# Attention and MLP kernel: keys and queries transposed by DMA from cast copies in DRAM, both halves of a head pair in one unit

## The chip, the cores and the metric

The kernel runs on one core of a Trainium2 chip. The metric is the device time of one execution in microseconds (us), the median over runs. Engines are named as in the profile: PE (TensorE, matmul), PEld (its weight loads), DVE (VectorE), ACT (ScalarE), POOL (GpSimd), SP (SyncE, which here only issues DMA transfers).

## The reference

```python
B, H, S, D = 8, 8, 576, 64            # q, k, v: float32
window = 32                           # 8 global tokens besides
mask = |pos_i - pos_j| <= window, or i global, or j global
attn = softmax(where(mask, q @ k.T / sqrt(D), -1e9))
x = (attn @ v).transpose(0, 2, 1, 3).reshape(4608, 512)
h = maximum(x @ w_in, 0)              # w_in 512 x 2048
out = (h * h) @ w_out                 # w_out 2048 x 512, float32 out
```

## The kernel before

A unit of attention is one pair of heads of one batch: 8 batches times 4 pairs, index `i = 4*b + hp`. Its 576 queries, with the 8 global queries repeated after each 144, make 608 columns; they are cut into two halves of 304. The keys stand in five tiles of 120 rows, each led by the 8 global keys. `WIN` lists for each half the windows (key tile, place in the score tile, first column, width) that the mask leaves: five in the first half, of which two have 8 columns and serve the global queries alone, and three in the second.

For one half, `scores` multiplies keys and queries into `sc` and takes the exponential on ACT; in batches 0 and 1 the mask is added by a matmul of `far` with the identity ahead of the scores, later it is a product on DVE (`er` to `et`). `pv` multiplies by the values and by ones into `acc` (sums beside outputs; in batches 0 and 1 in column tiles of 64), takes 1/sum on ACT as exp(-ln(sum)), and writes the scaled outputs to `xT` on DVE. The global queries' outputs of all four pairs are gathered in `gx`, and `scatter` copies them on POOL to their columns of `xT`, eight copies per batch.

Keys and queries come in natural order by `fetch_pair` (SP) in float32 to `st`, are cast to fp16 (`cast_tokens`, DVE and ACT) and transposed on PE with the identity (`transposed`), six transposes for each of k and q of a unit; DVE copies the result to `kt` and `qt`. Values come in float32 and are cast too (`cast_values`). The rows of global tokens come by an indirect DMA for two batches at a time (`gather_rows`), go to a DRAM scratch and from there under the tokens.

The MLP works on chunks of 512 tokens (columns of `xT`): `mm1` is one unit of four matmuls 128x512 with `w_in`, a relu on ACT and a square on DVE; `mm2` is a quarter of one output tile, four matmuls with `w_out`; after four quarters DVE copies `ot` and SP stores it. Chunk 0 has its first layer in two halves of 256 tokens (`mm1_half`, eight units each).

The order on every engine is the order in which the program is written. MLP units are laid between attention steps by `fill` and `take` from the list `fills`. Three PSUM buffers `mm`, one each of `sc`, `acc` and `tr`. Batch 0 runs all its first halves, then all second halves; from batch 2 on each half step has about two MLP units before and after the outputs of the half before. The last two chunks run alone at the end.

Of the kernel before, what the change touches and what calls it, by code (L numbers as in the profile page):

```python
# [17 lines left out]
KT = 120  # L18
NT = 5
# [15 lines left out]
SCW = (456, 440)  # L35
MB = (0, 456)
NBUF = 5
# [3 lines left out]
def kernel(  # L41
# [33 lines left out]
    bufs_of = {"sc": 1, "acc": 1, "tr": 1, "mm": 3}  # L75

# [3 lines left out]
    st = {nm: sbt("st" + nm, [TP + NG, H, TJ, D], FP32) for nm in "kq"}  # L80
    st["v"] = sbt("stv", [P, NT, H, D], FP32)
    kts = [sbt(f"kt{i}", [P, NT, P], FP16) for i in range(NBUF)]
    qts = [sbt(f"qt{i}", [P, NCOL], FP16) for i in range(NBUF)]

    vts = [sbt(f"vt{i}", [P, NT, 3, D], FP16) for i in range(NBUF)]
# [7 lines left out]
    nc.scalar.preload_act_table_set("natural_log_exp_and_others")  # L93


    g64 = sbt("g64", [1, NG], I64)
    src = {"k": k, "q": q, "v": v}
    gscr = {}

    def fetch_tokens(eng, nm, b, hp):  # L100
        hs = slice(2 * hp, 2 * hp + 2)
        eng.dma_start(
            out=st[nm][0:TP, hs].rearrange("p h j d -> p h (j d)"),
            in_=src[nm][b, hs].rearrange("h (p j) d -> p h (j d)", j=TJ),
        )

    def fetch_values(eng, b, hp):
        hs = slice(2 * hp, 2 * hp + 2)
        dst = st["v"]
        for h in range(2 * hp, 2 * hp + 2):  # L110
            eng.dma_start(
                out=dst[8 : 8 + KT, 0:4, h],
                in_=v[b, h, 0 : 4 * KT].rearrange("(t s) d -> s t d", s=KT),
            )
        eng.dma_start(
            out=dst[8 : 8 + KN[4], 4, hs], in_=v[b, hs, 4 * KT : S].rearrange("h s d -> s h d")
        )

    def fetch_globals(b, hp):
        def rows(nm):  # L120
            return gscr[(nm, b // 2)][b % 2, :, 2 * hp : 2 * hp + 2]


        for nm in "kq":
            js = range(TJ) if b == 2 else (TJ - 1,)
            for h in range(2):
                dst = st[nm][TP : TP + NG, 2 * hp + h, js[0] : TJ]
                nc.sync.dma_start(
                    out=dst, in_=rows(nm)[:, h].unsqueeze(1).to_broadcast((NG, len(js), D))
                )  # L130
        nc.sync.dma_start(
            out=st["v"][0:NG, :, 2 * hp : 2 * hp + 2].rearrange("p t h d -> p t (h d)"),
            in_=rows("v").rearrange("g h d -> g (h d)").unsqueeze(1).to_broadcast((NG, NT, 2 * D)),
        )

    fetch_tokens(nc.sync, "k", 0, 0)
    nc.scalar.dma_start(out=g64, in_=global_idx.unsqueeze(0))
    fetch_tokens(nc.scalar, "q", 0, 0)
    fetch_tokens(nc.scalar, "q", 0, 1)
    fetch_tokens(nc.sync, "k", 0, 1)  # L140
    fetch_values(nc.sync, 0, 0)
    fetch_values(nc.sync, 0, 1)
    fetch_tokens(nc.sync, "k", 0, 2)
    fetch_tokens(nc.sync, "q", 0, 2)
    fetch_values(nc.sync, 0, 2)
    fetch_tokens(nc.sync, "k", 0, 3)
    fetch_tokens(nc.sync, "q", 0, 3)
    fetch_values(nc.sync, 0, 3)


    idle = sbt("idle", [P, 512], FP16)
    nc.vector.memset(idle, 0.0)
    ones = sbt("ones", [1, P], FP16)
    nc.vector.memset(ones, 1.0)
    nc.scalar.copy(
        out=st["v"][0:NG].rearrange("p t h d -> p t (h d)"),
        in_=idle[0:NG].unsqueeze(1).to_broadcast((NG, NT, H * D)),
    )
    pidx = sbt("pidx", [P, 4], I32)
    nc.gpsimd.iota(pidx, pattern=[[0, 4]], base=0, channel_multiplier=1)  # L160
# [714 lines left out]
```

## Time and profile before

| | us |
|---|---|
| runs (three): median, lowest, highest | 371.36, 371.32, 372.39 |
| profiled execution: span, first to last instruction | 368.4 |
| PE busy / DVE busy / ACT busy / POOL busy | 347.7 / 250.5 / 249.2 / 51.3 |
| DMA: moved, mean rate | 43.93 MB, 119 GB/s |

The page gives for the profiled execution its own span and no separate time; the median of the runs lies 2.96 us above the span. Busy times of the engines overlap. A row of a timeline has the start, the busy time, the engine, the line and what was written from what; a matmul's busy time includes its passage through the array, so the price of a group on PE is read from the distance of starts. Names such as `mm<-xT,w_in` are output and inputs. In a table by stage the columns are the stage, its length, busy time of PE, PEld, DVE, ACT and POOL with instructions in brackets, the granted clock of PE, the DMA engines' busy share and GB/s.

### The profile page before, as it was taken

What the parts mean: (1) busy time and instruction counts of PE and PEld (TensorE: products, weight loads), DVE (VectorE), ACT (ScalarE), POOL (GpSimd) and SP (SyncE); (2) the same over time, 40 slices, a digit from 0 to 9 for tenths busy, and PEclk for the clock granted to TensorE, in tenths of its full rate; (3) what the DMA queues carried; (4) which work ended last, traced back from release to release, by engine and by line L of the source; (5) the groups of instructions that cost most, each with busy time, mean ns of one, the idle gap of its engine ahead of it and who ended that gap; (6) DMA issues with size and microseconds to landing.
All of it is one profiled execution on the core that took longest, in us unless ns stands there. A gap on an engine that the chain in (4) does not pass through costs nothing.

```text
span 368.4 us, 8258 instructions
## 1 busy us (share of the span) xinstructions
PE 347.7 (94%) x2941; PEld 186.0 (51%) x2941; DVE 250.5 (68%) x656; ACT 249.2 (68%) x482; POOL 51.3 (14%) x143
## 2 busy tenths in 40 slices
PE   7779799988899999999999999999999989999995
PEld 3556575544445555555555555555555544444442
DVE  7753566656888878977897789778977953422421
ACT  6656574465997799679967996799679942612610
POOL 5364430016000610020002000200020001000000
PEclk9978999998999999999999999999999999999999
DMA  8999999787843663375336533652020011002002
GB/s 196 192 147 201 193 228 201 188 188 193 188 130 97 188 166 94 90 188 142 95 93 187 142 95 93 187 140 60 30 87 2 0 52 64 0 30 85 0 32 85
DMA packets 65011, 43.93 MB, mean 119 GB/s; under 512 B 42730, under 2 KB 60074, under 8 KB 64970
## 3 DMA queue, kind: packets, MB, share of 16 engines
q1 hardware_dynamic: 59752, 38.03, 40.0%
q0 software_dynamic: 4800, 4.79, 7.9%
q10 hardware_dynamic: 418, 0.59, 0.7%
q8 instruction: 23, 0.38, 0.5%
q14 instruction: 18, 0.15, 0.1%
HBM read 37.85 MB, written 9.73 MB: 129 GB/s over the span
## 4 chain that ended last, share of the span: by engine, by line
PE 60%; issue 14%; DVE 7%; DMA 6%; ACT 5%; POOL 4%; POOLq 2%; ACTq 0%; SPq 0%; DVEq 0%
PE mm L502 25%; PE mm L460 24%; PE acc L602 4%; PE tr L415 3%; DMA w_in<-in_moe_w_in_dram 3%; PE sc L564 3%; DVE gt L466 2%; DMA stq<-in_q_dram 2%; POOLq L649 2%; ACT rl L465 2%; DMA stv<-in_v_dram 1%; POOL xT L658 1%; ACT er L570 1%; ACT natq L386 1%; DVE et L574 1%
## 5 line engine op out<-in xcount | busy, mean ns | idle before, releaser
L502 PE MATMUL mm<-w_out,gt 128*128 128x512 f16 x576 | 133.6, 379 | 0.0
L460 PE MATMUL mm<-xT,w_in 128*128 128x512 f16 x512 | 120.7, 382 | 1.0 <-POOL xT L658 1.0
L465 ACT ACTIVATE rl<-mm 128x512 f16<-128x512 f32 x128 | 72.2, 595 | 34.6 <-PE mm L460 33.9
L502 PEld LDWEIGHTS <-gt 128*128 128x128 f16 x576 | 53.1, 97 | 55.6
L460 PEld LDWEIGHTS <-w_in 128*128 128x128 f16 x512 | 47.7, 98 | 51.2 <-issue 2.9
L612 ACT ACTIVATE rec<-acc 64x288 f32<-64x288 f32 (+1 forms) x112 | 45.5, 406 | 33.9 <-PE acc L602 24.1
L638 DVE TENSOR_TENSOR xT<-acc,rec 64x288 f16<-64x288 f32 (+1 forms) x112 | 50.9, 454 | 19.8 <-ACT rec L613 18.0
L466 DVE TENSOR_TENSOR gt<-rl 128x512 f16<-128x512 f16 x128 | 50.2, 421 | 18.2 <-ACT rl L465 17.5
L658 POOL COPY xT<-gx 128x4 f16 (+2 forms) x80 | 21.8, 272 | 231.1 <-DVE xT L638 226.8
L570 ACT ACTIVATE er<-sc 128x912 f16<-128x912 f32 (+1 forms) x48 | 44.0, 917 | 5.4 <-PE sc L564 5.0
L574 DVE TENSOR_TENSOR et<-er,mask 128x912 f16<-128x912 f16 (+1 forms) x48 | 29.9, 623 | 21.2 <-ACT er L570 20.9
L508 DVE COPY ot<-mm 128x512 f32<-128x512 f32 x36 | 24.9, 691 | 26.0 <-PE mm L502 25.3
L613 ACT ACTIVATE rec<-rec 128x288 f32<-128x288 f32 x64 | 28.3, 443 | 2.0
L386 ACT CAST natq<-stq 104x768 f16<-104x768 f32 (+1 forms) x32 | 26.4, 824 | 4.4 <-DMA stq<-in_q_dram 4.4
L570 ACT ACTIVATE et<-sc 128x912 f16<-128x912 f32 (+1 forms) x16 | 14.6, 915 | 12.0 <-PE sc L564 11.7
L386 DVE CAST natk<-stk 104x768 f16<-104x768 f32 (+1 forms) x32 | 17.7, 552 | 0.3
L479 PE MATMUL mm<-xT,w_in 128*128 128x256 f16 x128 | 16.8, 290 | 0.6 <-POOL xT L658 0.6
L479 PEld LDWEIGHTS <-w_in 128*128 128x128 f16 x128 | 12.7, 104 | 3.3 <-issue 0.6
L617 DVE TENSOR_REDUCE gs<-acc 128x16 f32<-128x32 f32 x32 | 6.0, 187 | 12.2 <-ACT rec L612 12.2
L415 PE MATMUL tr<-identity,natk 96*128 96x96 f16 x168 | 12.1, 208 | 1.9 <-DVE natk L386 1.8
L415 PEld LDWEIGHTS <-natq 96*128 96x128 f16 x192 | 9.2, 98 | 7.1 <-ACT natq L386 1.5
L491 DVE TENSOR_TENSOR gt<-rl 128x512 f16<-128x512 f16 x16 | 6.8, 426 | 8.4 <-ACT rl L490 8.1
(205 smaller groups left out, 324.2 us busy)
## 6 DMA issues: line engine op xcount, KB each, us to landing
stk<-in_k_dram SPq DMA_DIRECT2D x32, 288.0 KB
out_dram<-ot SPq DMA_DIRECT2D x36, 256.0 KB
stq<-in_q_dram SPq DMA_DIRECT2D x30, 288.0 KB
stv<-in_v_dram SPq DMA_DIRECT2D x64, 120.0 KB
w_in<-in_moe_w_in_dram POOLq DMA_DIRECT2D x4, 512.0 KB, 9.5
w_out<-in_moe_w_out_dram POOLq DMA_DIRECT2D x4, 512.0 KB, 9.0
stv<-in_v_dram SPq DMA_DIRECT2D x32, 48.0 KB
stq<-in_q_dram ACTq DMA_DIRECT2D x2, 288.0 KB
```

Source lines behind the costliest of these rows:

```text
L386: op(out=nat[0:n].rearrange("p j (h d) -> p h j d", d=D), in_=st[nm][0:n, 2 * hp : 2 * hp + 2],)
L415: nc.tensor.transpose(tr[:, TP * j : TP * j + n], nat[0:n, j, :], identity[0:n, 0:n])
L460: nc.tensor.matmul(ph, w_in[:, t, u * P : (u + 1) * P], xT[:, t, XOFF + c * TC : XOFF + (c + 1) * TC], start=(t == 0), stop=(t == NDM - 1),)
L465: nc.scalar.activation(out=rl, in_=ph, func=AF.Relu)
L466: nc.vector.tensor_tensor(out=gts[c][:, u, :], in0=rl, in1=rl, op=ALU.mult)
L479: nc.tensor.matmul(ph[:, j], w_in[:, t, (u + j) * P : (u + j + 1) * P], xT[:, t, half * (256 + XOFF) : half * (256 + XOFF) + 256], start=( ...
L502: nc.tensor.matmul(po, gts[c][:, f, m * P : (m + 1) * P], w_out[:, f, :], start=(f == 0), stop=(f == NFF - 1),)
L570: nc.scalar.activation(out=er[:, :, 0:W], in_=sc[:, :, 0:W], func=AF.Exp, bias=0.0, scale=scale)
L574: nc.vector.tensor_tensor(out=et[:, :, 0:W], in0=er[:, :, 0:W], in1=mask[:, MB[half] : MB[half] + W].unsqueeze(1).to_broadcast((P, 2, W)), ...
L612: nc.scalar.activation(out=rec[r], in_=av[rs, xs, :, 0:GTOK], func=AF.Ln)
L613: nc.scalar.activation(out=rec, in_=rec, func=AF.Exp, scale=-1.0)
L638: nc.vector.tensor_tensor(out=xT[r, hp, x0 : x0 + HS].rearrange("p (k x) -> p k x", k=2), in0=av[r, x, :, 0:GTOK], in1=rec[r], op=ALU.mult,)
```

## The change

Windows, names and lines below are the changed kernel's. What it does:

- Batches 2 to 7: POOL issues casting transfers (float32 read, fp16 written). `tokens_to_scratch` rewrites keys and queries of a batch in DRAM in the padded order (five and four transfers, pieces of 64 numbers), `globals_to_scratch` puts the gathered global rows between them, and `transposes` (SP) brings them with two transposing transfers to `kb` and `qb`. The PE transposes, the casts and the copies to `kt` and `qt` are gone there. `values` fetches and casts values straight to `vb` (five transfers). All this for batch b+1 is written after the first unit of batch b; POOL reaches it when its scatter of batch b-1 is done.
- Batch 1: keys and queries come cast to `nat` by POOL and are transposed on PE, 12 transposes of one head each for each of k and q. Batch 0 loads keys and queries by SP alone, values cast by POOL.
- `WIN2` leaves the two 8-column windows out: from batch 1 on (and in batch 0's second half, where nothing changes by it) both halves have three windows. The global queries' sums are taken in both halves and added (`gsh`), so that `gx` follows the second half.
- The mask is a product on DVE, in place, except in batch 0's first half.
- `unit`: scores of both halves (PSUM `sc` and `acc`), both exponentials, both products, then MLP units, outputs of the first half into `sc`, MLP, outputs of the second into `acc`, MLP. Batch 0's first half runs all scores, then all outputs.
- The column numbers of the scatter are loaded by three instructions instead of 24; weights are no longer gated behind other transfers; the gather of batches 0 and 1 is issued before w_out.

ACT, in one stretch of the batches with MLP. Before (batch 2, first and second half of a pair):

```order
L465 ACTIVATE rl<-mm 128x512 x2
L612 ACTIVATE rec<-acc 64x288 x2
L613 ACTIVATE rec<-rec 128x288
L465 ACTIVATE rl<-mm 128x512 x2
L570 ACTIVATE er<-sc 128x2x440
L465 ACTIVATE rl<-mm 128x512 x2
L612 ACTIVATE rec<-acc 64x288 x2
L613 ACTIVATE rec<-rec 128x288
L465 ACTIVATE rl<-mm 128x512 x2
L386 CAST natq<-stq 104x2x6x64
L394 CAST vt_80<-stv 128x4x2x64
L394 CAST vt_80<-stv 104x2x64
```

And now, ACT over one whole unit (a pair, both halves) of batch 2:

```order
L592 ACTIVATE et<-sc 128x2x440
L592 ACTIVATE et<-acc 128x2x440
L492 ACTIVATE rl<-mm 128x512 x2
L648 ACTIVATE rec<-sc 64x288 x2
L649 ACTIVATE rec<-rec 128x288
L492 ACTIVATE rl<-mm 128x512
L648 ACTIVATE rec<-acc 64x288 x2
L649 ACTIVATE rec<-rec 128x288
L492 ACTIVATE rl<-mm 128x512 x4
```

The casts are gone, and the two exponentials stand back to back ahead of the unit's relus.

SP, the transfers between two stores of outputs in batch 2, before (one pair's loads, of which there are four a batch):

```order
L102 DMA stk<-in_k_dram 96x2x384
L102 DMA stq<-in_q_dram 96x2x384
L111 DMA stv<-in_v_dram 120x4x64 x2
L115 DMA stv<-in_v_dram 96x2x64
L128 DMA stk<-gscr_k_1964 8x64 x2
L128 DMA stq<-gscr_q_1966 8x64 x2
L131 DMA stv<-gscr_v_1968 8x5x128
L510 DMA out_dram<-ot 128x512 x2
```

And now, SP for a whole batch (`scr` is the DRAM copy, `gst` the gathered rows):

```order
L378 DMA scr_k_710<-gstk 64x5x64
L378 DMA scr_q_713<-gstq 64x4x64
L355 DMA gscr_v_2047<-gstv 64x64
L401 DMA_TRANSPOSE kb<-scr_k_710 128x4x640
L401 DMA_TRANSPOSE qb<-scr_q_713 128x4x608
L410 DMA vb_77<-gscr_v_2047 8x8x64 x5
L537 DMA out_dram<-ot 128x512 x4
```

The stores of a chunk now stand behind the next batch's transposing transfers, which wait for POOL's.

POOL, around the scatter of batch 0's second half, with the semaphores that each waits for (DMASW: an earlier POOL transfer in the same of eight lanes). Before, ahead of it:

```order
L735 COPY xT<-xT 128x4x32 [waits Pool_49]
L754 COPY w_out<-w_in 1x1 [waits DMASW3_49,Pool_49]
L756 DMA w_out<-in_moe_w_out_dram 128x4x512 [waits Pool_49]
L756 DMA w_out<-in_moe_w_out_dram 128x4x512 x3
L649 TENSOR_LOAD g32b [waits DVE_49]
```

And now, up to that scatter's first copy (`vb_689` is batch 1's values):

```order
L761 COPY xT<-xT 128x4x32 [waits Pool_49]
L106 DMA natk<-in_k_dram 96x4x384 [waits DMASW0_49]
L106 DMA natq<-in_q_dram 96x4x384 [waits DMASW1_49]
L106 DMA natk<-in_k_dram 96x4x384 [waits DMASW2_49]
L106 DMA natq<-in_q_dram 96x4x384 [waits DMASW3_49]
L341 DMA gstk<-in_k_dram,gidx 128x64 [waits DMASW4_49]
L341 DMA gstq<-in_q_dram,gidx 128x64 [waits DMASW5_49]
L341 DMA gstv<-in_v_dram,gidx 128x64 [waits DMASW6_49]
L113 DMA vb_689<-in_v_dram 120x8x64 [waits DMASW7_49]
L113 DMA vb_689<-in_v_dram 120x8x64 [waits DMASW0_49]
L695 ISA
L695 COPY xT<-gx 128x4 [waits DVE_49,Pool_49]
```

The lanes go round: the last transfer here waits for the first `natk` of the same list, and the copy stands behind it. The weights' transfers lie ahead of all these in POOL's queue.

The diff, cut to what the prediction speaks of:

```diff
+WIN2 = (
+    ((0, 0, 0, 160), (1, 160, 88, 192), (2, 352, 216, 88)),
+    ((2, 0, 304, 112), (3, 112, 344, 192), (4, 304, 472, 136)),
+)
...
+    pool, dve, act = nc.gpsimd, nc.vector, nc.scalar
+    nat = {nm: sbt("nat" + nm, [TP + NG, H, TJ, D], FP16) for nm in "kq"}
...
+    def fetch_values(b, x, hs=slice(0, H)):
+        back = NG if b == 0 and x else 0
+        pool.dma_start(
+            out=vb[b][NG - back : NG + KN[x], x, 2 * hs.start : 2 * hs.stop : 2],
+            in_=v[b, hs, x * KT - back : x * KT + KN[x]].rearrange("h s d -> s h d"),
+        )
...
+    def globals_to_scratch(b):
+        for nm in "kq":
...
+            nc.sync.dma_start(
+                out=dst.rearrange("x g h d -> (g h) x d"),
+                in_=gathered(nm, b).unsqueeze(1).to_broadcast((NG * H, n, D)),
+            )
+        store_rows("v", b)
+
+    def tokens_to_scratch(b):
+        for nm in "kq":
+            n, step, pitch, off = {"k": (NT, KT, P, NG), "q": (4, GTOK, GRP, 0)}[nm]
+            for x in range(n):
+                lo, hi = x * step, min((x + 1) * step, S)
+                pool.dma_start(
+                    out=scr[(nm, b % 2)][x * pitch + off : x * pitch + off + hi - lo].rearrange(
+                        "s (h d) -> s h d", d=D
+                    ),
+                    in_=src[nm][b, :, lo:hi].rearrange("h s d -> s h d"),
+                )
+
+    def transposes(b):
+        for nm, d_, w in (("k", kb, KW), ("q", qb, QW)):
...
+            nc.sync.dma_start_transpose(out=d_[b], in_=scr[(nm, b % 2)][:, :])
...
+    def weights(half, sc, wins, added=False):
+        W = sum(x[3] for x in wins[half])
+        et = sbt("et", [P, 2, SCW[0]], FP16, bufs=4)
+        act.activation(
+            out=et[:, :, 0:W], in_=sc[:, :, 0:W], func=AF.Exp, bias=0.0, scale=scale
+        )
+        if not added:
+            dve.tensor_tensor(
+                out=et[:, :, 0:W], in0=et[:, :, 0:W],
...
-    for half in range(2):
-        for u in range(0, NFF, 2):
-            fills.append((8 * half + 8, 2, mm1_half, (u, half)))
+    half1(0)
+    half1(1)
+    for i in range(0, NHP, 2):
+        for nm in "kq":
+            fetch_tokens(pool, nm, 1, i, 2)
...
+    gather(1)
+    globals_to_scratch(2)
+    for x in range(2):
+        fetch_values(1, x)
+    keep_warm(4)
+    half1_out(0)
+    half1_out(1)
+    queue += units[0]
+    take(2)
+    half1(2)
+    half1(3)
+    take(2)
+    half1_out(2)
+    take(1)
+    half1_out(3)
+    take(3)
     scatter(0, 1)
+    for x in range(2, NT):
+        fetch_values(1, x)
+    tokens_to_scratch(2)
+    transposes(2)
...
+    queue += units[1] + units[2]
+    take(6)
...
+    def unit(i, n, nxt=None):
+        scs = [scores(i, half, pair_tag[half], WIN2) for half in range(2)]
+        et = [weights(half, scs[half], WIN2) for half in range(2)]
+        take(n[0])
+        if nxt:
+            tr_k(nxt, tag="tr", tail=act.copy)
+            tr_q(nxt, tag="mm", op=act.copy)
         for half in range(2):
+            acc = outputs(i, half, et[half], pair_tag[half], WIN2, columns=i < 2 * NHP)
+            finish_outputs(i, half, acc, columns=i < 2 * NHP)
+            if half == 0:
+                take(n[1])
+        if i % NHP == NHP - 1:
+            scatter(i // NHP)
+        take(n[2])
+
+    for hp in range(NHP):
+        unit(NHP + hp, (1, 1, 2) if hp < NHP - 1 else (1, 1, 2), NHP + hp + 1 if hp + 1 < NHP else None)
+    take(99)
+    for b in range(2, B):
+        queue += units[b + 1]
+        for hp in range(NHP):
+            unit(NHP * b + hp, ((2, 1, 4), (2, 1, 4), (2, 1, 5), (2, 1, 7))[hp])
+            if hp == 0 and b + 1 < B:
+                if b > 2 and b % 2:
+                    gather((b + 1) // 2)
+                globals_to_scratch(b + 1)
+                tokens_to_scratch(b + 1)
+                transposes(b + 1)
+                vb[b + 1] = vb[(b + 1) % 2]
+                values(b + 1)
+                value_globals(b + 1)
+        take(99)
+    queue += units[B + 1] + units[B + 2]
+    take(999)
```

More of the change, by code (lines that the diff above doesn't have):

```diff
@@ L136 @@
[L136 to L148, printed above, removed]
+            fetch_tokens(nc.sync, nm, 0, hp)
@@ new lines, in mask_first, with scores @@
+    def mask_first(half, tag):
+        sc = pst(tag, [P, 2, 512])
+        W = SCW[half]
+        for e in range(2):
+            nc.tensor.matmul(
+                sc[:, e, 0:W], identity, far[:, 0:W],
+                start=True, stop=False, skip_group_check=True,
+            )
+        return sc
+    def scores(i, half, tag, wins, sc=None):
+        kt, qt = key_query(i)
+        added = sc is not None
+        if not added:
+            sc = pst(tag, [P, 2, 512])
+        for t, so, c0, w in wins[half]:
@@ new lines, with half1, half1_out @@
+    scatter(0, 0)
+    pool.tensor_copy(out=xT[:, :, XOFF + 256 : XOFF + HS], in_=xT[:, :, 256:HS])
+    def half1(i):
+        tag = pair_tag[i % 2]
+        ets[i] = weights(1, scores(i, 1, tag, WIN2), WIN2)
+    def half1_out(i):
+        acc = outputs(i, 1, ets[i], pair_tag[i % 2], WIN2, columns=True)
+        finish_outputs(i, 1, acc, columns=True)
+    half1(0)
+    half1(1)
+    for i in range(0, NHP, 2):
+        for nm in "kq":
+            fetch_tokens(pool, nm, 1, i, 2)
+    vb[1] = sbt("vb1", [P, NT, 2 * H, D], FP16)
```

576 lines of the change are left out of this document (243 added, 333 removed).

## The prediction

> **What bounds the kernel now.** I read the page's busy line first, then a table by stage, then TensorE's own order of time in one steady stretch, then the chain that ended last.
>
> ```profile
> PE 347.7 (94%) x2941; PEld 186.0 (51%) x2941; DVE 250.5 (68%) x656; ACT 249.2 (68%) x482; POOL 51.3 (14%) x143
> PE 60%; issue 14%; DVE 7%; DMA 6%; ACT 5%; POOL 4%; POOLq 2%; ACTq 0%; SPq 0%; DVEq 0%
> 159.00:196.00 37.00, 36.73 (x307) 19.27 (x305) 30.67 (x77) 30.66 (x61) 2.53 (x9) 1.00 0.50 132
> 158.78 2.90 POOL L658 COPY xT<-gx 128x4 f16 x8 [26.88 <-DVE xT L638]
> 195.68 2.89 POOL L658 COPY xT<-gx 128x4 f16 x8 [33.99 <-DVE xT L638]
> ```
>
> In the stage 159 to 196 TensorE (PE) is busy 36.73 of 37.00 us, VectorE (DVE) and ScalarE (ACT) some 30.7, and the DMA engines half. The scatters of two neighbouring batches lie 36.90 us apart: that is one batch, and TensorE sets it. Here is what it runs in it; the start of a row less the start of the one before is that one's price.
>
> ```profile
> 171.82 0.40 PE L564 MATMUL sc<-qt_76,kt_71 64*128 64x160 f16 x10
> 172.15 0.43 PE L415 MATMUL tr<-identity,natk 96*128 96x96 f16 x6
> 172.42 1.89 PE L460 MATMUL mm<-xT,w_in 128*128 128x512 f16 x8
> 174.15 0.54 PE L602 MATMUL acc<-et,vt_80 128*128 128x112 f16 x6
> 174.53 1.91 PE L460 MATMUL mm<-xT,w_in 128*128 128x512 f16 x8
> 176.37 0.36 PE L564 MATMUL sc<-qt_76,kt_71 64*128 64x112 f16 x6
> 176.67 0.43 PE L415 MATMUL tr<-identity,natq 96*128 96x96 f16 x6
> 176.94 1.89 PE L460 MATMUL mm<-xT,w_in 128*128 128x512 f16 x8
> 178.67 0.63 PE L602 MATMUL acc<-et,vt_81 128*128 128x160 f16 x10
> 179.15 1.89 PE L460 MATMUL mm<-xT,w_in 128*128 128x512 f16 x8
> ```
>
> Eight MLP matmuls cost 1.73 us, so a unit of four costs 0.866. Scores cost 0.33 (ten matmuls) and 0.30 (six), outputs 0.48 and 0.38, six transposes 0.27. A pair of heads takes 0.33+0.30+0.48+0.38+0.54 = 2.03 us, four pairs 8.1; 32 MLP units 27.7; together 35.8 of 36.9.
>
> **The steady batches (2 to 7).** The transposes leave TensorE, and both halves have six matmuls, so a pair costs 2x0.30+2x0.38 = 1.36 us and a batch 4x1.36+27.7 = 33.1. Next I ask what is late then. A pair with seven first-layer units costs TensorE 7x0.866+1.36 = 7.42 us. ACT's rows, and one of a last output:
>
> ```profile
> 167.04 1.07 ACT L465 ACTIVATE rl<-mm 128x512 f16<-128x512 f32 x2
> 168.00 0.91 ACT L570 ACTIVATE er<-sc 128x880 f16<-128x880 f32 x1
> 168.85 0.60 ACT L465 ACTIVATE rl<-mm 128x512 f16<-128x512 f32 x1
> 170.34 0.82 ACT L612 ACTIVATE rec<-acc 64x288 f32<-64x288 f32 x2
> 171.19 0.44 ACT L613 ACTIVATE rec<-rec 128x288 f32<-128x288 f32 x1
> 171.54 0.58 ACT L465 ACTIVATE rl<-mm 128x512 f16<-128x512 f32 x1
> ...
> 192.78 0.55 PE L602 MATMUL acc<-et,vt_82 128*128 128x112 f16 x6
> ```
>
> By starts: exponential 0.85, relu 0.48, a pair of logarithms 0.85, reciprocal 0.35. The pair costs ACT 2x0.85+7x0.48+2x0.85+2x0.35 = 7.46: even with TensorE. ACT starts the two exponentials only after the last relu of the pair before, so I allow 0.35 us of waiting to each of the two such pairs: 7.8. The other two pairs hold 8 and 10 units, mostly second-layer ones without a relu: 8.3 and 10.0. A batch is 2x7.8+8.3+10.0 = 33.9 us. The casts of queries, keys and values leave ACT and DVE, which wait on TensorE there, and count nothing. The scatter now follows both halves: from the end of a last output (192.78+0.55) to the scatter (195.68) it is 2.35 us now, on ACT and DVE, and 2.90 on POOL; seven units, 6.1 us, and the next scores, 0.6, cover these 5.25. Without that cover they would be lost in each batch.
>
> **What feeds them.** For each batch from 2 on POOL issues 14 casting transfers: nine that rewrite keys and queries in fp16 in DRAM, 9216 pieces of 256 bytes read and 128 written, and five of values, 4608 pieces. SP then issues two transposing transfers of 1.28 MB in all. No row shows either kind; these are the nearest.
>
> ```profile
> q1 hardware_dynamic: 1642, 0.42, 120.8%
> q0 software_dynamic: 1639, 1.63, 123.3%
> L705 POOL DMA_DIRECT2D w_in<-in_moe_w_in_dram x4: 755/851/1246, 18.6 to 21.5; - x4
> L756 POOL DMA_DIRECT2D w_out<-in_moe_w_out_dram x4: 750/759/770, 33.3 to 35.5; - x4
> L375 POOL DMA_DIRECT2D gscr_k_1067<-gstk x1: 580/580/580, 49.8 to 49.8; - x1
> DMA packets 3378, 2.00 MB, mean 249 GB/s; under 512 B 2477, under 2 KB 3315, under 8 KB 3378
> ```
>
> The first row is the stretch 7 to 9 us, nearly all 256-byte pieces of values: 821 a us with all engines busy. The second is 22 to 30 us, weights cast from 2048 to 1024 bytes: 205 a us. The last is 48 to 56 us, at 249 GB/s. By these 13,824 pieces take 16.8 us at the first pace and 67 at the second. I take the first: its pieces read the same 256 bytes, the second row's eight times as many. The transposes take 5.1 us at 249 GB/s, and 24 as 4992 pieces of 256 bytes at the weights' pace; I take 5.1, the row nearest in mixed sizes. The four outputs of a batch (1.05 MB) take 4.2, the copies of global rows 0.7. Sum 26.8 of 33.9 us: hidden. On POOL an issue costs 0.58 us for 128 pieces and 0.76 for 512, 0.5 ns a piece; for about 990 pieces 1.0, so 14 cost 14 us, which start right behind the scatter and end 15 us before the next. The keys' transfers should land some 9 us into a batch and the queries' 14; if the transposes are late, the next batch's scores wait, and so do the output stores queued behind them on SP. SP itself issues 15 transfers a batch instead of 40. The Trainium skill (DMA: Bandwidth & Descriptors, "Latency and other measured facts") gives a transposing transfer 261 GB/s, by which the pair would be an estimated 4.9 us and the sum 26.6; no run here shows it yet.
>
> **The front.** The second chunk's MLP begins at 84.19 us now. These rows price the way to it:
>
> ```profile
> 26.46 4.27 PE L479 MATMUL mm<-xT,w_in 128*128 128x256 f16 x24 [0.64 <-POOL xT L658]
> 49.80 0.57 PE L594 MATMUL acc<-et,vt_82 128*64 128x112 f16 x12
> 50.31 3.67 PE L479 MATMUL mm<-xT,w_in 128*128 128x256 f16 x32
> 53.81 1.03 PE L502 MATMUL mm<-w_out,gt 128*128 128x512 f16 x4
> 84.19 3.54 PE L460 MATMUL mm<-xT,w_in 128*128 128x512 f16 x8 [0.99 <-POOL xT L658]
> 40.56 2.87 POOL L658 COPY xT<-gx 128x4 f16 x8 [4.28 <-DVE xT L638]
> ```
>
> The new thing there is a wait on POOL. Every POOL transfer waits for the eighth transfer before it (POOL's rows in the part on the change), so the second transfer of batch 1's values waits for the first one of batch 1's keys, which stands behind both weights in the same queue, and the scatter of batch 0's second half stands behind it. Time until those keys land: start 2 us, keys and queries of batch 0 2.36 MB at 249 GB/s 9.5, values 5.6, 4096 weight pieces at 205 a us 20.0, gathers 0.5, the keys themselves 1.4, some 2 to land: 41. One issue more and the scatter, 1+3: 45. Now it ends at 43.4. Behind it: eight half units of 0.875 us (32 matmuls in 3.50) 7.0, and 1.7 for a cold clock (84.19 took 3.54 for eight, 172.42 took 1.89); transposes of the first pair 1.08 (24 of 64 rows each: between 0.54, as 12 now, and 1.08, if each costs as one now; I take the upper, as the columns that stream are the same); two units 1.73: 56.5. A pair of batch 1 then costs scores 0.60, outputs in column tiles 2x0.51, four units 3.46, transposes 1.08 = 6.2, the last 3.4: 22.0, to 78.5. No MLP unit is left to cover the scatter of batch 1, so TensorE waits 2.35 us for ACT and DVE and 2.9 for the scatter: 83.7. I take 83.5, about the present place, give or take 6: nothing is won ahead of it. The rest of the front's edits (scores and outputs of batch 0 in two loops, masks by product instead of by matmul, constants moved from POOL to DVE) I cost at nothing, and what hides them is the same queue: the first scatter stands behind w_out's fourth part, which waits for w_in's third (2+9.5+5.6+7.5+2 = 27), and ends near 31, later than the work before it (26.46 now); from there TensorE has 7.0+1.7+1.6 us of work, to 41, and then waits for 45. Beyond these 4 us each would count in full.
>
> **The sum.** From the start of the second chunk: six batches 203.4, less scores already run 0.6, plus 1.7 cold clock: 204.5. Then 64 units for the last two chunks, and the end:
>
> ```profile
> 309.36 13.81 PE mm L460 x64
> 350.80 13.83 PE mm L502 x64
> 364.65 0.69 DVE ot L508
> ```
>
> Four times 13.82 is 55.3, and from the last matmul to the end of the span, 368.4, 3.7. In all 83.5+204.5+59.0 = 347.0 of span. The page gives its execution's span only; the median of the runs, 371.36, lies 3.0 above it, which I add: **350 us**, 21 less than now, all from the steady batches.
>
> **Rivals.** (1) The casting path bounds the batch. For it: 13,824 small pieces and a copy through DRAM that the kernel never made. Against it: 821 pieces a us. It decides where pieces cost over 1.6 times that row (27.4 us, with 10 of other transfers in the 37.4 us that a batch may last before 21 us are lost); at twice, 33.6+10 = 43.6 a batch, the time is 350+6x9.7 = 408. (2) Only the 9216 pieces written to DRAM in 128 bytes cost double: 22.5+5.6+10 = 38.1 a batch and 375. The Trainium skill (DMA: Bandwidth & Descriptors, "Specifications") says that pieces below 512 bytes are read, modified and written; the 256-byte row above shows no such price for SBUF, and none here shows DRAM. (3) The transposes take 24 us instead of 5.1: 45.7 a batch and 421; it decides past 15.7 for the pair. For it: no row shows one. Against it: 249 GB/s for mixed plain transfers. (4) ACT's order, with two exponentials back to back, costs a further 0.5 us in each of 24 pairs: 362. For it: ACT's 7.46 us are TensorE's 7.42. (5) POOL's issues starve beside DVE's copies. The weight issues spread from 755 to 1246 ns, 1.65 times, by which 14 take 23 us, still ahead of the scatter; past twice the scatter is late, at five times (70 us) a batch is 73 and the time 585. The Trainium skill (SBUF — State Buffer, "A bandwidth-pool intuition that's wrong (but worth ruling out)") has 620 ns grow to 3100 beside a DVE copy; the trace agrees in sign alone, and DVE's steady work after the change is products and copies out of PSUM. (6) Steady batches as long as now, for a cause unseen: no change.
>
> **How the numbers follow.** About 0.3%, 1.1 us, can be told from no change. My forecast, 343 to 358, has 0.48; rival 4 or a front 6 us later, to 368, 0.16; less than 343 0.06; so faster 0.70. Rival 6 has 0.04. Rival 2 has 0.09, 1 has 0.08, 3 has 0.06, 5 has 0.03: slower 0.26. The range from 340 to 384 leaves out 0.02 below and 0.16 above (1, 3 and 5).
>
> **What would show it.** Right: scatters 33 to 35 us apart from batch 2 on, with TensorE above 95% there; the transposing rows landing before two thirds of a batch; POOL idle ahead of each scatter; the second chunk at 78 to 90. Wrong: scores (L583) that wait for kb or qb; casting transfers below 500 pieces a us; output stores late on SP; scatters that wait for POOL's own issues. The costliest error would be the price of 128-byte pieces written to DRAM.

## The result and the profile after

The changed kernel takes **347.21 us** (median of four runs, 347.08 to 347.38); the kernel before took 371.34 on the same chip (four runs, 371.01 to 372.39). The ratio is 0.934, 95% interval 0.931 to 0.937: 24.1 us less. The forecast was 350.0, between 340 and 384.

The page of the changed kernel, its busy line, the chain that ended last and POOL's DMA queue:

```profile
span 345.7 us, 6663 instructions
...
PE 323.3 (94%) x2377; PEld 167.2 (48%) x2377; DVE 211.6 (61%) x534; ACT 212.0 (61%) x422; POOL 125.6 (36%) x211
...
q0 software_dynamic: 105056, 17.42, 66.5%
...
PE 59%; ACT 14%; issue 11%; POOL 8%; DVE 5%; DMA 2%; POOLq 0%; ACTq 0%
```

TensorE still fills 94% of a span that is 22.7 us shorter. ACT and DVE lost 37 and 39 us of work each, and yet ACT's share of the chain that ended last rose from 5% to 14%: a first sign that it comes next. POOL's queue carries 105,056 packets; the feed of batches 2 to 7, six times 13,824 small pieces, is four fifths of them.

One steady batch: POOL's scatters, then TensorE's second pair of it (by starts), then all four pairs by windows. A window's third number from the end is the granted clock; the DMA share behind it adds up the times of all packets, and passes 1 where packets overlap.

```profile
148.79 2.07 POOL L695 COPY xT<-gx 128x4 f16 x8 [14.89 <-DVE xT L676]
182.64 2.05 POOL L695 COPY xT<-gx 128x4 f16 x8 [18.99 <-DVE xT L676]
```

```profile
158.76 0.36 PE L583 MATMUL sc<-qb,kb 64*128 64x160 f16 x6
158.96 0.35 PE L583 MATMUL acc<-qb,kb 64*128 64x112 f16 x6
159.25 1.90 PE L487 MATMUL mm<-xT,w_in 128*128 128x512 f16 x8
160.99 0.55 PE L625 MATMUL sc<-et,vb 128*128 128x160 f16 x6
161.37 1.03 PE L487 MATMUL mm<-xT,w_in 128*128 128x512 f16 x4
162.23 0.55 PE L625 MATMUL acc<-et,vb 128*128 128x112 f16 x6
162.62 2.75 PE L487 MATMUL mm<-xT,w_in 128*128 128x512 f16 x12
165.70 1.02 PE L487 MATMUL mm<-xT,w_in 128*128 128x512 f16 x4 [0.33 <-ACT rl L492]
166.66 0.36 PE L583 MATMUL sc<-qb,kb 64*128 64x160 f16 x6
```

```profile
151.10:158.76 7.66, 7.52 (x53) 3.72 (x53) 5.82 (x14) 7.13 (x14) 7.54 (x10) 1.00 1.47 124
158.76:166.66 7.90, 7.57 (x54) 3.77 (x54) 6.15 (x16) 7.62 (x15) 4.89 (x6) 1.00 2.02 158
166.66:174.92 8.26, 8.26 (x57) 4.14 (x57) 5.90 (x14) 5.68 (x11) 0.00 (x0) 1.00 1.42 151
174.92:184.91 9.99, 9.99 (x65) 4.95 (x65) 6.03 (x15) 4.21 (x8) 1.62 (x8) 1.00 0.22 82
```

The scatters lie 33.85 us apart, 36.90 before. Only scores, outputs and MLP units are left on TensorE. In the third and fourth pair it is busy all the time; in the first two it waits, 0.33 us in the second with ACT's relu named, and ACT's busy time there (7.62 of 7.90) is the highest of the four.

Two places of the front, TensorE behind batch 0's second scatter and behind batch 1's:

```profile
42.86 9.14 PE L506 MATMUL mm<-xT,w_in 128*128 128x256 f16 x56 [3.43 <-POOL xT L695]
82.49 3.20 PE L487 MATMUL mm<-xT,w_in 128*128 128x512 f16 x8 [2.49 <-POOL xT L695]
```

The second chunk's MLP begins at 82.49, 84.19 before. Read from the chain, the span goes 82.5 to there, 204.05 to the two last chunks (286.54; 225.17 before) and 59.15 for these. So 21.1 us of the 22.7 come from batches 2 to 7 and 1.7 from the front.

### The profile page after: what moved, and what is told of

It is laid out like the page before. It is cut to its first block, busy times and chain, and to the rows that moved or that the text cites. A ratio compares the mean times of both kernels' runs of the same rounds, so it can differ in the third digit from the quotient of the medians.

```text
span 345.7 us, 6663 instructions
## 1 busy us (share of the span) xinstructions
PE 323.3 (94%) x2377; PEld 167.2 (48%) x2377; DVE 211.6 (61%) x534; ACT 212.0 (61%) x422; POOL 125.6 (36%) x211
## 3 DMA queue, kind: packets, MB, share of 16 engines
q0 software_dynamic: 105056, 17.42, 66.5%
## 4 chain that ended last, share of the span: by engine, by line
PE 59%; ACT 14%; issue 11%; POOL 8%; DVE 5%; DMA 2%; POOLq 0%; ACTq 0%
PE mm L529 32%; PE mm L487 18%; ACT rl L492 6%; ACT et L592 3%; POOL vb L113 3%; ACT rec L648 3%; DMA vb<-in_v_dram 2%; PE mm L506 2%; POOL xT L695 2%; DVE xT L676 2%; PE sc L625 2%; PE sc L583 1%; PE acc L625 1%; DVE gt L493 1%; ACT rec L649 1%
## 5 line engine op out<-in xcount | busy, mean ns | idle before, releaser
L592 ACT ACTIVATE et<-sc 128x880 f16<-128x880 f32 (+1 forms) x32 | 29.0, 905 | 44.9 <-PE sc L583 34.9
L596 DVE TENSOR_TENSOR et<-et,mask 128x880 f16<-128x880 f16 x60 | 37.0, 617 | 29.7 <-ACT et L592 29.7
L113 POOL DMA_DIRECT2D vb<-in_v_dram x40 | 42.6, 1733 | 1.5 <-DMA w_out<-in_moe_w_out_dram 1.0
L676 DVE TENSOR_TENSOR xT<-sc,rec 64x288 f16<-64x288 f32 (+1 forms) x56 | 25.5, 455 | 9.2 <-ACT rec L649 8.1
L592 ACT ACTIVATE et<-acc 128x880 f16<-128x880 f32 (+1 forms) x32 | 29.0, 907 | 1.7 <-PE mm L425 1.1
L676 DVE TENSOR_TENSOR xT<-acc,rec 64x288 f16<-64x288 f32 (+1 forms) x56 | 25.5, 455 | 5.3 <-ACT rec L649 4.8
L648 ACT ACTIVATE rec<-sc 64x288 f32<-64x288 f32 (+1 forms) x56 | 22.8, 407 | 7.5 <-PE sc L625 4.2
L625 PEld LDWEIGHTS <-vb 128*128 128x128 f16 x288 | 21.7, 99 | 11.7 <-issue 0.5
L389 POOL DMA_DIRECT2D scr_k<-in_k_dram x30 | 26.6, 1118 | 1.2 <-issue 1.2
L389 POOL DMA_DIRECT2D scr_q<-in_q_dram x24 | 25.4, 1697 | 0.0
L648 ACT ACTIVATE rec<-acc 64x288 f32<-64x288 f32 (+1 forms) x56 | 22.6, 404 | 1.8 <-PE acc L616 0.6
```

The source lines that it names most:

```text
L113: pool.dma_start(out=vb[b][NG - back : NG + KN[x], x, 2 * hs.start : 2 * hs.stop : 2], in_=v[b, hs, x * KT - back : x * KT + KN[x]].rearra ...
L389: pool.dma_start(out=scr[(nm, b % 2)][x * pitch + off : x * pitch + off + hi - lo].rearrange("s (h d) -> s h d", d=D), in_=src[nm][b, :, l ...
L592: act.activation(out=et[:, :, 0:W], in_=sc[:, :, 0:W], func=AF.Exp, bias=0.0, scale=scale)
L596: dve.tensor_tensor(out=et[:, :, 0:W], in0=et[:, :, 0:W], in1=mask[:, MB[half] : MB[half] + W].unsqueeze(1).to_broadcast((P, 2, W)), op=AL ...
L625: nc.tensor.matmul(acc[:, e, o : o + w], vtf[:, t, vo : vo + P], et[:, e, so : so + w], start=(n == 0), stop=(n == nw - 1), skip_group_che ...
L648: act.activation(out=rec[r], in_=av[rs, xs, :, 0:GTOK], func=AF.Ln)
```

## Experiments

Each kernel is the changed one with the edit shown. They ran on three chips, on which the medians of the kernel before lie between 367.5 and 370.7 us; so times are compared as ratios to it (the changed kernel: 0.934), and steady batches by the distance from the scatter of batch 3 to that of batch 4. That distance varies far less than the whole time: it is 33.85 in the changed kernel and in each of the three that change only what comes ahead of these batches.

**Is the feed hidden? Without it from batch 4 on.**

```diff
+                if b + 1 < 4:
                     globals_to_scratch(b + 1)
                     ...
                     value_globals(b + 1)
```

> For batches 4 to 7 nothing is brought in any more: no casting transfers, no transposing transfers, no rows of global values (attention works on what the buffers hold from two batches before). Theory (the feed is hidden and takes nothing from TensorE or ACT): within 0.7 us of 347.2. Rival (the feed costs steady time through something shared, such as late output stores or slower copies): at least 0.5 us less in each of four batches, 345 or below; a steady batch then falls from 33.85 us.

It took 346.63 us, a ratio of 0.938 (0.935 to 0.942).

```profile
114.80 2.04 POOL L695 COPY xT<-gx 128x4 f16 x8 [21.14 <-DVE xT L676]
148.65 2.04 POOL L695 COPY xT<-gx 128x4 f16 x8 [27.52 <-DVE xT L676]
```

From 114.80 on POOL brings nothing any more, and the five distances from there are 33.85 and four times 33.84 us. The 14 casting transfers, their 12.4 us of POOL and the two transposing transfers cost a steady batch nothing.

**Where does it stop being hidden? Keys and queries rewritten twice and three times.**

```diff
-                tokens_to_scratch(b + 1)
+                for _ in range(2):           # 3 in the other kernel
+                    tokens_to_scratch(b + 1)
```

> Keys and queries of batches 3 to 7 are rewritten twice, 9216 pieces more a batch, 23,040 in all. Theory, by the pace of the changed kernel's row from 158 to 159.5 us (1821 packets in 1.5 us, 1214 a us): 19.0 us, with 10 us of other transfers 29 of 33.85: hidden, within 1 us of 347.2. Rival, by the prediction's pace (821 a us): 28.1 with 10 others 38.1 a batch, 4.2 over, five times: some 368.

> As before, three times: 32,256 pieces a batch. By 1214 pieces a us 26.6 us, with 10 us of other transfers 36.6: 2.7 over the batch, five times: 361. By 821 a us 39.3 and 49.3 in all: 15.4 over, five times: 424. If POOL's issues set it instead (32 of them, 12.4 us for 14 now, so 28): hidden, 347.

Twice: 356.16 us, a ratio of 0.965 (0.960 to 0.970). Three times: 381.44 us, 1.033 (1.024 to 1.043). Both lie between what the two paces gave. From batch 2's scatter on the distances are, twice, 33.85, 38.76, 34.94, 37.61 and 33.91 (9.8 us over five steady batches), and three times 45.7, 40.2, 41.6, 44.2 and 37.7 (40 over). What TensorE and DVE wait for, from the tables of waits of the two kernels (us in total, times, longest), with twice first:

```profile
PE sc L583 <- DMA qb<-scr_q: 5.6, 2, 3.3
DVE ot L535 <- DMA out_dram<-ot: 13.9, 3, 7.4
```

```profile
PE sc L583 <- DMA qb<-scr_q: 14.3, 4, 7.1
DVE ot L535 <- DMA out_dram<-ot: 45.4, 5, 13.1
```

These are the two rows that the prediction named for a feed that comes late: scores that wait for `qb`, and stores of outputs that stand on SP behind the transposes. The feed decides at less than 23,040 pieces, 1.67 times the 13,824 of the change. The theory of hidden pieces at 1214 a us fell too. In the kernel with three, what follows the scatter at 111.46 ends so, on SP's queue (SPq) and on TensorE:

```profile
145.99 5.37 SPq L401 DMA_TRANSPOSE kb<-scr_k  x1
151.58 5.93 SPq L401 DMA_TRANSPOSE qb<-scr_q  x1
```

```profile
160.43 0.37 PE L583 MATMUL sc<-qb,kb 64*128 64x160 f16 x6 [0.90 <-DMA qb<-scr_q]
```

So the scores wait at the end of a chain: POOL's issues, the landing, and two transposes one after the other. But from 112 to 159 us the DMA engines are also nine tenths busy or more in nearly all of the time: the transfers together take longer than each one's best pace gives. Which of the two weighs more, the chain or the sum, no run separates.

**What are the transposes worth? Put back on TensorE, of an old tile.**

```diff
         take(n[0])
+        if i >= 2 * NHP:
+            for _ in range(2):
+                tr = pst("tr", [P, 1024], FP16)
+                for j in range(TJ):
+                    nc.tensor.transpose(tr[:, TP * j : TP * j + TP],
+                        nat0[("k", NHP - 1)][:, j, :], identity[0:TP, 0:TP])
```

> Twelve transposes of 96x96 a pair are put back on TensorE in batches 2 to 7 (of an old tile; nobody reads the result), nothing else changes. Their price before was 0.27 us for six. Theory (TensorE sets the third and fourth pair of a batch, ACT the first two, which leave TensorE 0.22 and 0.48 us): 24 x 0.54 = 13.0 less 6 x 0.7 = 4.2, so 8.8 more: 356.0. Rival (TensorE sets all pairs): 13.0 more, 360.2.

It took 359.49 us, a ratio of 0.974 (0.971 to 0.978). The number is the rival's, but the rows are the theory's with a dearer price. Its pairs one, two and three:

```profile
153.51:161.64 8.13, 8.07 (x65) 4.34 (x65) 5.82 (x14) 7.13 (x14) 7.99 (x11) 1.00 1.51 125
161.64:169.77 8.13, 8.07 (x65) 4.34 (x65) 6.16 (x16) 7.61 (x15) 4.42 (x6) 1.00 2.01 141
169.77:178.77 9.00, 8.94 (x70) 4.74 (x70) 5.91 (x14) 5.67 (x11) 0.00 (x0) 1.00 1.28 143
```

```profile
155.74 0.89 PE L823 MATMUL tr<-identity,nat0k 96*128 96x96 f16 x12
156.46 0.55 PE L625 MATMUL sc<-et,vb 128*128 128x160 f16 x6
```

Twelve transposes in a row take 156.46 - 155.74 = 0.72 us, not twice the 0.27 of six. Its pair starts at 153.51, so these two rows lie in the first window. The third pair grows by all of it (8.26 to 9.00); the first two only to 8.13, which is TensorE's 7.42 and 0.72: the waits in them are gone. Four times 0.72 less 0.75 of waits is the 2.13 us by which the scatters moved apart (35.98), 12.8 us in six batches. So the first two pairs of the changed kernel had that much room on TensorE.

**And the 8-column windows? Five windows in the first half again.**

```diff
+        W = (WIN[0] if i >= 2 * NHP else WIN2[0], WIN2[1])
-        scs = [scores(i, half, pair_tag[half], WIN2) for half in range(2)]
+        scs = [scores(i, half, pair_tag[half], W) for half in range(2)]
...                                       # W likewise in weights and outputs
```

> In batches 2 to 7 the first half has its two windows of 8 columns again: eight matmuls more a pair on TensorE, 16 score columns more on ACT and DVE (the global queries' sums are then not those of the reference). By the prediction's price 0.13 us a pair. Theory (first two pairs set by ACT's queue): 2 x 0.13 a batch, and 0.03 for wider exponentials: scatters 34.1 to 34.2 apart, 2 us more in all. Rival (TensorE sets all four): 34.4, 3.1 more.

The ratio is 0.945 (0.940 to 0.951), and the scatters are 34.24 us apart: 0.39 more, 2.3 in six batches. That lies between the two, nearer to the theory. Its four pairs take 7.76, 7.92, 8.42 and 10.14 us: the third and the fourth grew by 0.16 and 0.15, a little over the price of 0.13, the first two by 0.10 and 0.02.

Put back one at a time, the transposes and the windows make up 2.13 + 0.39 = 2.52 of the 3.05 us by which a batch became shorter. No run puts back the casts and copies of ACT and DVE or the old order of the two halves, so what those are worth stays open.

**What makes TensorE wait in the first two pairs: ACT's order or its load?** ACT's rows of the second pair:

```profile
159.36 0.90 ACT L592 ACTIVATE et<-sc 128x880 f16<-128x880 f32 x1
160.15 0.91 ACT L592 ACTIVATE et<-acc 128x880 f16<-128x880 f32 x1
160.93 1.11 ACT L492 ACTIVATE rl<-mm 128x512 f16<-128x512 f32 x2
162.06 0.82 ACT L648 ACTIVATE rec<-sc 64x288 f32<-64x288 f32 x2
...
165.07 2.29 ACT L492 ACTIVATE rl<-mm 128x512 f16<-128x512 f32 x4
167.25 0.90 ACT L592 ACTIVATE et<-sc 128x880 f16<-128x880 f32 x1
```

ACT works from 159.36 to 167.25, 7.89 us, without a gap. Two relus take 162.06 - 160.93 = 1.13, four 2.18 and the single one between 0.61: seven take 3.92, 0.56 each, where the prediction had 0.48. The first test changes the order alone, the next two the load.

```diff
-        et = [weights(half, scs[half], WIN2) for half in range(2)]
-        take(n[0])
+        et = [weights(0, scs[0], WIN2)]
+        take(1)                          # batches 2 to 7
+        et.append(weights(1, scs[1], WIN2))
+        take(n[0] - 1)
```

> In batches 2 to 7 one first-layer unit stands between the two exponentials; ACT's work is the same. By the prediction's reason for 0.35 us a pair (the exponentials stand back to back behind the last relu) it would win up to 0.7 us a batch: 343.0. If ACT's load sets these pairs: within 1 us of 347.2.

```diff
+        if u in (4, 11):                 # (2, 9) in the other kernel
+            nc.vector.tensor_scalar(out=rl, in0=ph, scalar1=0.0, scalar2=None, op0=ALU.max)
+        else:
             nc.scalar.activation(out=rl, in_=ph, func=AF.Relu)
```

> Two of a chunk's 16 relus, the fifth and the twelfth, which lie in the two pairs of a batch that hold seven first-layer units, go from ACT to DVE. Theory (ACT's load sets these pairs: 7.64 and 7.90 us where TensorE has 7.42 of work): both fall to 7.42, 0.7 us a batch, 4.2 in six: 343.0. Rival (the order, two exponentials back to back, sets them): the wait moves, within 1 us of 347.2. Below that: DVE becomes late and the pairs lengthen, above 348.

> As the kernel that gave two relus of a chunk to DVE, but the third and the tenth: the one unit between the two outputs of a pair, where DVE has an idle stretch, instead of one behind the last outputs, where DVE still writes xT (there the relu started 0.5 us after its unit was done and TensorE waited for the bank). Theory (ACT's queue, without a gap for 7.89 us in the first two pairs, sets them): without one relu of 0.56 it has 7.33, TensorE's 7.42 set the pair, scatters 33.85 - 0.7 = 33.1 us apart, 4 us less in all. Rival (any relu moved makes DVE late, since its products wait in the same queue): 33.9 to 34.1 apart, no gain.

Exponentials apart: ratio 0.943 (0.940 to 0.946), scatters 34.58 apart: 0.7 us a batch worse. The second exponential now comes behind another relu, the second outputs start 0.18 us later behind the first ones, and ACT's second pair grows from 7.89 to 8.06 us. Relus on DVE: 0.939 (0.934 to 0.944) with 34.04 apart, and 0.946 (0.941 to 0.951) with 34.36. None gained. DVE in the first of these two, and TensorE in the second:

```profile
157.67 0.92 DVE L679 TENSOR_TENSOR xT<-acc,rec 64x288 f16<-64x288 f32 x2 [0.20 <-ACT rec L652]
158.62 0.43 DVE L496 TENSOR_TENSOR gt<-rl 128x512 f16<-128x512 f16 x1
159.08 0.69 DVE L493 TENSOR_SCALAR rl<-mm 128x512 f16<-128x512 f32 x1
```

```profile
157.91 1.89 PE L487 MATMUL mm<-xT,w_in 128*128 128x512 f16 x8 [0.39 <-DVE rl L493]
```

A relu in DVE's queue stands behind the writing of `xT`, which waits for ACT; its PSUM bank comes free later than ACT would have freed it, and TensorE waits for DVE instead. These two say nothing against ACT's load, since ACT now idles (0.5 us) for want of input; they only show that DVE's queue is no better place.

**Cold clock and the wait for batch 1's scatter.** Two ways to fill TensorE's waits in the front: idle matmuls, or real units held back.

```diff
     take(3)
+    keep_warm(13)                        # idle matmuls alone
     scatter(0, 1)
...
+        scs = [scores(i, 0, "sc", WIN2)]
+        if i == 2 * NHP: keep_warm(6)    # held units: take(2)
+        scs.append(scores(i, 1, "acc", WIN2))
+        if i == 2 * NHP: keep_warm(9)    # held units: take(1)
...                                       # from here held units alone
-        unit(NHP + hp, (1, 1, 2) if hp < NHP - 1 else (1, 1, 2), ...
+        unit(NHP + hp, (1, 1, 1) if hp < NHP - 1 else (1, 1, 0), ...
-    take(99)
```

> Idle matmuls fill TensorE's two waits for a scatter: 13 ahead of the one at 42.86 us, six and nine around the scores at 79.63. Granted clock is 0.50 from 42.86 to some 48.7 us and from 82.49 to some 86.3. Theory (the idle time lets the clock fall): 2.9 and 1.9 us come back, 342.4. Rival (the clock falls for the kind of work or at that time anyway): 347.2.

> Three second-layer units of chunk 0 are held back from batch 1 and run in the waits for batch 1's last outputs and its scatter (1.61 and 2.49 us). Theory (TensorE sets batch 1's pairs, so each unit held back shortens them by 0.866): 2.6 us less, and part of the 1.9 of cold clock behind: 343.0 to 344.6. Rival (batch 1's pairs are set by ACT and DVE and do not shorten): 347.2.

Idle matmuls: ratio 0.930 (0.929 to 0.932), 345.16 us. Held units: 0.924 (0.922 to 0.926), 342.36 us. The 56 matmuls behind batch 0's second scatter, in the kernel with held units (where nothing ahead of them was changed), in the one without feed, and with idle matmuls:

```profile
43.05 6.27 PE L506 MATMUL mm<-xT,w_in 128*128 128x256 f16 x56 [3.33 <-POOL xT L695]
```

```profile
42.80 7.86 PE L506 MATMUL mm<-xT,w_in 128*128 128x256 f16 x56 [2.96 <-POOL xT L695]
```

```profile
45.90 6.27 PE L506 MATMUL mm<-xT,w_in 128*128 128x256 f16 x56
```

Without idle matmuls, the same 56 matmuls behind nearly the same wait took 9.14 us in the changed kernel, 6.27 and 7.86 in the first two of these. With idle matmuls the clock stayed at 1.00, but a wait of 3 us does not always let it fall. Behind batch 1's scatter the traces agree better: the first eight matmuls took 3.20 to 3.57 us in all nine kernels (the changed one among them) that leave the wait there empty, and 1.89 in all four that fill it, with idle matmuls or with units. So there it is the empty wait that costs the clock, not the time or the kind of work.

The idle matmuls still missed their 342.4. In the profiled execution the clock was at 0.50 from 20.3 to 34.0 us already, ahead of the edit, and the first scatter came 2.1 us later than in the changed kernel (29.71, 27.62). From there to batch 2's scatter it won 3.3 us (83.98, 87.32 in the changed one).

Part of the gain of the kernel with held units (scatter of batch 0's second half to that of batch 1's 35.55 us, 39.00 in the changed one) is therefore luck, 2.9 us of clock in its profiled execution; from that scatter to the next it won 2.2 us more (33.12, 35.30 in the changed one), which is the wait filled and the cold clock behind it gone. Without that luck the three units won some 2.8 us (39.00 - 35.55 - 2.87 + 2.18). Batch 1's pairs shrank by 1.1 us for 2.6 of units taken out: TensorE sets them only in part.

**Held units, nine idle matmuls, and values issued behind the scatter.**

```diff
     globals_to_scratch(2)
-    for x in range(2):
-        fetch_values(1, x)
...
     take(3)
+    keep_warm(9)
     scatter(0, 1)
-    for x in range(2, NT):
+    for x in range(NT):
         fetch_values(1, x)
...                                       # and the held units as above
```

> The held-back units (three of chunk 0's second layer in the waits for batch 1's scatter), nine idle matmuls ahead of batch 0's second scatter, and all five transfers of batch 1's values issued behind that scatter. Theory: the scatter starts when DVE is done, 0.94 us earlier than at 40.64; the clock stays at 1.00 behind it (0 to 2.9 us, since it did not always fall); with the held units' own gain a ratio near 0.917 to the kernel before, 340 us. Rival (the scatter then waits for another lane, or the first feed of batch 2 comes late): no better than the held units alone, 0.924.

339.15 us, a ratio of **0.919** (0.914 to 0.924). POOL in the changed kernel:

```profile
38.48 0.99 POOL L113 DMA_DIRECT2D vb<-in_v_dram  x1 [1.02 <-DMA w_out<-in_moe_w_out_dram]
39.71 0.94 POOL L113 DMA_DIRECT2D vb<-in_v_dram  x1 [0.23 <-DMA natk<-in_k_dram]
40.64 2.17 POOL L695 COPY xT<-gx 128x4 f16 x8
```

And here POOL's scatter, and TensorE behind the idle matmuls:

```profile
37.71 2.51 POOL L695 COPY xT<-gx 128x4 f16 x8 [0.80 <-DVE xT L676]
```

```profile
40.66 6.28 PE L506 MATMUL mm<-xT,w_in 128*128 128x256 f16 x56
```

From the first scatter to this one it is 10.64 us, 13.02 in the changed kernel: 2.38 less, where 0.94 was expected, and the scatter waits for DVE again, not for POOL's own transfers. It now starts 0.14 us behind DVE's last `xT` instead of 0.94 us (40.64 behind 39.70), which is 0.80 of the 2.38; for the rest, DVE itself is done 1.58 us earlier after the first scatter, and why it is stays open. It beats both kernels of the case: the interval does not touch that of the changed kernel.

**A fourth bank.** On top of that, the MLP takes the PSUM bank of the transposes.

```diff
-        ph = pst("mm", [P, 512])
+        ph = pst("tr" if u % 4 == 3 else "mm", [P, 512])
...                                       # likewise one tile of the second layer
```

> The kernel with held-back units, idle matmuls and late values, and besides a fourth PSUM bank for the MLP from chunk 1 on: the bank of the transposes, which no batch from 2 on uses, takes every fourth first-layer unit and the last second-layer tile of a chunk. Theory (TensorE waits where three banks are full and ACT still has the relu of the first to do; in the third pair ACT has 5.68 us of work in 8.26 and catches up): the wait of 0.33 us goes and scatters come 33.1 to 33.5 us apart, 336 to 338 in all (a ratio of 0.910 to 0.915). Rival (ACT's queue of 7.89 us sets the first two pairs, whatever the banks: the exponentials then come late and the outputs wait): 33.85 apart, no change to 0.919.

337.77 us, a ratio of 0.919 (0.913 to 0.925): the same, within what these runs can tell. The scatters are 33.64 apart, 0.21 less: between the theory's 33.1 to 33.5 and the rival's 33.85. Its first three pairs, and where the third waits:

```profile
141.52:148.92 7.40, 7.40 (x53) 3.75 (x52) 5.52 (x13) 6.86 (x14) 7.25 (x9) 1.00 1.37 117
148.92:156.51 7.59, 7.57 (x54) 3.78 (x54) 5.95 (x15) 7.41 (x16) 5.20 (x6) 1.00 2.11 162
156.51:165.18 8.67, 8.43 (x59) 4.15 (x58) 6.41 (x15) 6.16 (x12) 0.00 (x0) 1.00 1.65 153
```

```profile
159.14 0.54 PE L625 MATMUL sc<-et,vb 128*128 128x160 f16 x6 [0.24 <-DVE et L596]
```

With a bank more TensorE runs the first pair at its own 7.40, the second nearly so, and pays 0.41 in the third, where the outputs wait for a late exponential: ACT's own pairs stay 7.81 and 7.80 us (its exponentials start at 141.93, 149.74 and 157.54). That speaks for load and against the banks: ACT's 7.8 us set the first two pairs, and the banks mostly decide where TensorE waits for them. No run took work off ACT without making another engine late, so this is argued from the rows and not shown by a faster kernel.

## Why the prediction was right

The forecast's span was 347.0; it is 345.7. Almost all of the gain came where the forecast put it, in the steady batches; that the total is so close is partly luck, since several terms were off in opposite directions. By its own steps:

- **Steady batches: right, 33.9 predicted, 33.85 measured**, pair by pair 7.8, 7.8, 8.3 and 10.0 against 7.66, 7.90, 8.26 and 9.99. The reason for the first two was half right. ACT does set them, as far as the runs above go, but the 0.35 us was not a wait of stacked exponentials: ACT's own pair is 7.89 and not 7.46, since seven relus took 3.92 instead of 3.36 (and the two exponentials 1.57 instead of 1.70). Setting the exponentials apart made it worse. Of the 3.05 us by which a batch became shorter, 4 x 0.67 = 2.7 are, by the prediction's prices, the work taken off TensorE; the rest is less waiting, 1.1 a batch before (35.8 of 36.9) and 0.75 now (33.1 of 33.85). Rival 4 (362) fell: no pair lost a further 0.5 us.
- **The feed: hidden, as predicted, with terms wrong that nearly cancel.** Once under way the casting transfers ran faster than predicted, and the transposes slower. The DMA queue of POOL from 158.0 to 159.5 us (packets, MB, share), when the writes still went to DRAM and the casts had the DMA engines nearly to themselves, and SP's rows:

```profile
q0 software_dynamic: 1821, 0.23, 240.2%
```

```profile
159.89 4.84 SPq L401 DMA_TRANSPOSE kb<-scr_k  x1
164.96 6.74 SPq L401 DMA_TRANSPOSE qb<-scr_q  x1
```

  1821 packets in 1.5 us are 1214 a us, 1.48 times the 821 of the prediction: 13,824 take 11.4 us at that pace, not 16.8. That is the best stretch: ahead of it, from 152.7 to 158.0, beside a store and the global rows, 4022 packets took 5.3 us, 2.0 more than at that pace. From 164.0 to 173.2, 9.2 us, the casts had 3904 packets left, 3.2 us at that pace; that leaves 6.0 for 4535 of the 4992 packets of the transposes, an estimated 6.6 for all, not 5.1. In all the transfers ran with hardly a gap from 152.7 to 173.2, 20.5 us, against 16.8 + 5.1 = 21.9 predicted. They landed at 173, 72% of the batch, a little past the two thirds of the prediction, and 11.7 us ahead of the scores that need them (184.91). POOL's 14 issues took 12.4 us (14 predicted), and POOL then idled 19 us ahead of its scatter (15 predicted).
- **Rivals 1 to 3 and 5 fell.** Pieces written to DRAM in 128 bytes show no double price: 1214 of them a us. The Trainium skill (DMA: Bandwidth & Descriptors, "Specifications") has transfers below 512 bytes read, modified and written; the trace shows no doubled price from it, since these go faster than the 821 a us of 256-byte pieces to SBUF. The point from which the feed decides cannot be read from such a sum, though: at 1.67 times the pieces it gives a loss of 4.2 us a batch by the prediction's pace and none by the measured one, and 2.0 were measured. The sum leaves out that the transposes follow one another on SP behind the last landing, and that transfers beside each other take longer: from 166 to 171 us of the changed kernel 3472 packets of casts and 1345 of transposes took 5.0 us, where the casts' 1214 a us and the 1086 of the transposes alone (172 to 173) would make an estimated 4.1.
- **The front: right to 1 us, out of errors of both signs.** Predicted 83.5, measured 82.49. The first scatter ended at 30.42 (near 31), the second at 42.81 (45: batch 1's keys landed by 39.7, not 41). The cold clock behind it cost 2.9 us instead of 1.7. Transposes of a pair took 0.56 us, the lower end of the range and not the upper 1.08 that was taken; batch 1's four pairs still took 22.15 (22.0), since TensorE waits there, twice 0.43 us for DVE's `xT` among others. The new wait on POOL's own queue was there (0.94 us from DVE's last `xT` to the scatter), and taking it away is part of the faster version. That the errors cancel is luck.
- **Tail and end: 59.15 against 59.0.**
- **What lies around the span: 3.0 added, 1.7 measured** (347.38 for the profiled execution with its span of 345.7). This was the largest single error of the sum. The 3.0 set the median of some executions against the span of another; in later executions of the kernel before, time and span lie 1.9 to 2.1 apart.

## What to carry to other kernels

Work that an engine does only to bring data into shape is worth as much as that engine is late in that stage, and the waits of the stage's next engine are taken off it: price the pair by both engines' queues, relus and all, before counting a win in full. For a feed that is to stay hidden, the sum of its transfers at the best pace seen is too small a bound: follow also its longest chain from trigger to need, and double one link to see the margin in one run. And look at the waits of the front for work that can be held back: three units moved by a few lines gave 2.8 us, 0.8%, apart from the luck with the clock.

## What the chip showed that was not expected

- Casting transfers of small pieces are quick: 1214 packets a us, 256 bytes read and 128 written each, over 1.5 us in which they had the DMA engines nearly to themselves.
- A transposing transfer keeps SP's queue busy, 4.84 us for 640 rows and 6.74 for 608 while casting transfers run; plain transfers of SP in the same kernel show 0.3 to 1.5.
- Transposes on TensorE that write 64 rows follow at some 23 ns each (12 in 0.28 us), those that write 128, in a run of twelve, at 60 ns (0.72 us).
- After a wait of 3.0 to 3.4 us TensorE's clock fell to 0.50 for 5.9 us in the changed kernel, for less in others and not at all in two (waits of 3.22 and 3.33 us). Two waits of 2.44 us at the same place cost nothing, and waits of 4.14 and 4.65 us cost 2.7 and 2.5 us. The Trainium skill (TensorE: Matmul & The Clock Gate, "What's actually happening") says that the gate watches a free-running window of about 3.4 us; waits just at that length that cost 0 to 2.9 us agree with it.
